# Reordering the first 512 tokens of a fused scan, expert and feed-forward kernel, with dummy matmuls between

## Chip, cores and metric

One core of a Trainium2 chip. The metric is device microseconds of one execution of the program. Engines are named as in the profile: PE (TensorE), DVE (VectorE), ACT (ScalarE), POOL (GpSimd), SP (SyncE, which here only issues DMAs).

## What is computed

```python
# attention-like scan: B, H, S, D = 4, 8, 768, 48
scale = np.minimum(mag, 0.999) / (mag + 1e-06)
for t in range(S):
    new_re = ar * S_re - ai * S_im
    new_im = ar * S_im + ai * S_re
    S_re, S_im = (new_re + kv, new_im)          # kv = outer(k, v)
    y[:, :, t] = np.einsum('bhd,bhde->bhe', q[:, :, t], S_re)
# x: 3072 tokens of 384; E = 4 experts of 1024
for e in range(E):
    h = np.maximum(x @ w1[e], 0.0)
    out += p[:, e:e + 1] * (h @ w2[e])
# second network, hidden 2048
h = x @ w_in
return np.maximum(0.01 * h, h) @ w_out
```

## The kernel before, in words

**Chunks.** The scan is cut into 24 chunks of 128 tokens, six for each batch. A chunk has two generators, and each call of `next` on one issues a few instructions. `elementwise(c)` (L163) has 18 calls: DVE, ACT and POOL turn the decays into running magnitudes (the scans at L198 and L203), running phases (L216) with sine and cosine, and the tile `ft`, the products with q and k (L234, two multiplies). Its last call, `by_head` (L243), issues six DMAs that turn `ft` into `hd`, which has the heads' features in partitions. `products(c)` (L258) has eight calls: PE transposes k (`pt`, L269; copied to `kt`, L270), multiplies scores (`sc`, L280; DVE masks them into `att`, L281), makes the next state (`pm`, L289; DVE writes `st`) and the output (`py`, L301 and, for a chunk with a state before it, L303), which ACT copies to `y` and PE transposes once more (`px`, L311). ACT and DVE then split `px` into `xh` and `xl` (L319, L320), a rounded part and the rest. All small tiles of PSUM here (`pt`, `sc`, `pm`, `py`, `px`) turn through two buffers of one tag, so each waits for the reader of the one before the last.

**Units.** Four chunks are a group of 512 tokens, and six groups go through 32 units of the experts and 16 of the second network. A unit is 128 hidden columns. `gemm_in` (L444) issues nine matmuls into `ph`; DVE makes `hp` (L460), ACT `hh` (L472), DVE `hl` (L473); `gemm_out` (L476) issues nine more into `acc` (L484 to L486). `ph` has three buffers, so a `gemm_in` waits for the `hp` of three units earlier. I call nine matmuls on one set of tokens a piece. Group 0 is special: its first `NHALF` units run on 256 tokens (chunks 0 and 1), then again on the other 256 (chunks 2 and 3), and only the rest on all 512. A unit's weights come raw and are split in two (`wt`): for the first six halves by PE (`rest_early`, two matmuls with the identity, L429 and L430), later by ACT and POOL (L408, L409). SP stores split weights to HBM (`ws`) and reads them back for every later use.

**What sets the order.** Each engine executes its instructions in the order in which they were issued, and that order is written by hand. Before the first unit a string, `PLAN`, is read letter by letter: a digit is one step of that chunk's `elementwise`, `p` and `q` one step of the products of chunks 0 and 1, `s` and `m` the two parts of the early weight split, `n` the normalisation of the expert weights. After it, the unit loop (L609 on) issues for unit number s: `gemm_in` of s + 2, some steps of `background()`, `split_h` of s + 2, `gemm_out` of s, more background steps. `background` finishes the `elementwise` steps of chunks 2 and 3, idles `WAIT` steps, runs the products of chunks 2 (`r`) and 3 (`t`), and goes on with chunk 4 and later. `pace` says how many steps are due by when; `KN` and `E2` set its first slope.

Of the kernel before, what the change touches and what calls it, by code (L numbers as in the profile page):

```python
# [10 lines left out]
F32 = mybir.dt.float32  # L11
# [21 lines left out]
AR_MIN = 0.76  # L33
NHALF = 8
PLAN = (
    "0101001010101011" "01ss0000mm" "00sss11mm000" "1111ppsm23111qq"
    "23232n3pp23p2ppqq3q23qqpq23m"
)
MAXT = 3
KN = 3.0  # L40
PT = 32
TPOOL = 6
MARGIN = 2.0
LAG = 2
E2 = 20
RAWS = 4
# [5 lines left out]
NSTEPS = ESTEPS + len(PSTEPS)  # L52
WAIT = 4
AR_MAX = 1e4
# [7 lines left out]
def fused_kernel(  # L62
# [20 lines left out]
    with ExitStack() as fast:  # L83
# [74 lines left out]
        def table(name):  # L158
            if tables[0] != name:
                A.preload_act_table_set(name)  # L160
                tables[0] = name

        def elementwise(c):  # L163
            t, vt = inputs[c]
# [78 lines left out]
        def by_head(c):  # L243

            ft, vt = feats[c]
            pool = p_el2 if c in (1, 3) else p_el
            hd = pool.tile([2 * D, H, 2 * P + 1], F32, name="hd")
            for ri in range(2):
                for i in range(NG):
                    row = ri * D + i * DG  # L250
                    (A if c < 2 and (i == ri or i == 2 - ri) else SP).dma_start(hd[row : row + DG], ft[:, ri, i])
            feats[c] = (ft, hd, vt)
# [5 lines left out]
        def products(c):  # L258
# [7 lines left out]
            for ri in range(2):  # L266
                pt = ps_a.tile([P, NG, P], F32, name="pt", tag="pa")
                for i in range(NG):
                    PE.transpose(pt[:, i], ft[:, ri, i, P : 2 * P], ident)  # L269
                A.copy(  # L270
                    kt[:, :, ri * D : (ri + 1) * D].rearrange("t h (r d) -> t r d h", d=DG),
                    pt.rearrange("t r (d h) -> t r d h", h=H),
                )
                yield
# [25 lines left out]
            for h in range(H):  # L300
                PE.matmul(py[:, h], att[:, h], vt[:, h * D : (h + 1) * D], start=True, stop=first)  # L301
                if not first:
                    PE.matmul(py[:, h], hd[:, h, :P], old[:, h], start=False, stop=True)  # L303
                if h == 3:
                    yield
# [182 lines left out]

        def zipped(*gens):
            gens = list(gens)  # L490
            while gens:
                for x in list(gens):
                    if next(x, gens) is gens:
                        gens.remove(x)
                yield

        def run_all(*gens):
            gens = list(gens)
            while gens:
                gens = [x for x in gens if next(x, gens) is not gens]  # L500

        with tc.manual_schedule():
# [13 lines left out]
            early_halves = iter([(s, part) for s in range(6) for part in (0, 1)][: PLAN.count("s")])  # L516
            for x in PLAN + "m" * 8:
                if x in steps:
                    next(steps[x], None)
                elif x == "n":  # L520
                    normalise_probs()
                    load_pb(0)
                elif x == "s":
                    cast_early(*next(early_halves))
                elif x == "m":
                    rest_early()
            for s in (5, 6):
                load_unit(s)
            split_unit(3, 0)

            def background():
                for _ in range(2):
                    next(steps["2"])
                    yield
                for _ in zipped(steps["2"], steps["3"]):
                    yield
# [36 lines left out]

            first = 2 + max(0, ESTEPS + 1 - min(PLAN.count("2"), PLAN.count("3"))) + WAIT + E2 - PLAN.count("r") - PLAN.count("t")
            pace = [(0.0, 0), (KN, first)]
# [267 lines left out]
```

## Time and profile before

| | us |
|---|---|
| three runs, median (lowest to highest) | 1477.9 (1477.68 to 1480.69) |
| the profiled execution: its own time | 1478.36 |
| its span in the trace | 1476.6 |
| PE busy in the span | 1402.4 (95%) |
| DVE / ACT / POOL busy | 864.7 / 564.8 / 264.5 |

PE's busy time counts a matmul as busy whether the clock is at its full 2.4 GHz or at 1.2 GHz; the granted clock (PEclk, 1.00 or 0.50) says which. Time is lost for PE both where it stands idle and where it is busy at 0.50.

### The profile page before, as it was taken

The numbers are of one execution on the slowest core, as the hardware profiler recorded it, in microseconds if no ns is written. First come the engines' busy times: TensorE is split into PE (matmuls) and PEld (weight loads), VectorE is DVE, ScalarE is ACT, GpSimd is POOL, SyncE is SP. The second block draws the span as 40 slices with busy tenths as digits, with TensorE's granted clock in tenths as the row PEclk, the third lists the DMA queues.
The fourth block names the chain that finished last, engine by engine and source line by source line (L and its number), as shares of the span: only waits on it lengthen the run. The fifth ranks groups of instructions, "written<-read, shape, count | busy, mean of one in ns | idle before, by whom it ended". The sixth has DMA issues, their size and how long they took to land.

```text
span 1476.6 us, 18540 instructions
## 1 busy us (share of the span) xinstructions
PE 1402.4 (95%) x6978; PEld 1177.2 (80%) x6978; DVE 864.7 (59%) x1504; ACT 564.8 (38%) x961; POOL 264.5 (18%) x244
## 2 busy tenths in 40 slices
PE   3858999999999999999999999999999999999997
PEld 1858888888777888788888888888888888888886
DVE  7556887788988898785454554554443333333332
ACT  5424565444345434455234354233332111323232
POOL 2120565412223223221011110110110000100000
PEclk9569999999999999999999999999999999999999
DMA  7288789986788789588567477576465665556561
GB/s 192 43 207 301 212 255 298 331 291 208 273 301 290 250 305 319 153 303 245 153 234 222 151 242 216 188 222 199 154 199 172 231 207 196 190 188 208 190 212 65
DMA packets 91043, 325.49 MB, mean 220 GB/s; under 512 B 10464, under 2 KB 32064, under 8 KB 90944
## 3 DMA queue, kind: packets, MB, share of 16 engines
q1 hardware_dynamic: 87488, 318.71, 67.1%
q10 hardware_dynamic: 3456, 5.51, 1.3%
q8 instruction: 56, 0.92, 0.3%
q14 instruction: 43, 0.35, 0.1%
HBM read 262.72 MB, written 42.52 MB: 207 GB/s over the span
## 4 chain that ended last, share of the span: by engine, by line
PE 58%; DVE 2%; ACT 0%; issue 0%; DVEq 0%; ACTq 0%
PE ph L455 27%; PE acc L484 9%; PE acc L486 9%; PE acc L485 9%; PE sc L280 1%; PE py L301 1%; PE py L303 1%; PE pm L289 1%; PE pt L269 0%; DVE hl L473 0%; DVE hp L460 0%; PE px L311 0%; DVE d L349 0%; ACT hh L472 0%; DVE d L355 0%
## 5 line engine op out<-in xcount | busy, mean ns | idle before, releaser
L455 PE MATMUL ph<-xh,wt 128*128 128x512 f32 (+1 forms) x1200 | 397.9, 388 | 0.0
L484 PE MATMUL acc<-hh,wt 128*128 128x512 f32 (+1 forms) x888 | 350.8, 395 | 5.2 <-ACT o L604 5.1
L486 PE MATMUL acc<-hl,wt 128*128 128x512 f32 (+1 forms) x888 | 342.9, 386 | 4.5 <-DVE hl L473 4.5
L485 PE MATMUL acc<-hh,wt 128*128 128x512 f32 (+1 forms) x888 | 341.5, 385 | 0.0
L472 ACT CAST hh<-hp 128x512 fp32r<-128x512 f32 (+1 forms) x296 | 180.4, 610 | 418.2 <-DVE hp L460 326.5
L473 DVE TENSOR_TENSOR hl<-hp,hh 128x512 fp32r<-128x512 f32 (+1 forms) x296 | 213.4, 721 | 150.3 <-ACT hh L472 149.1
L455 PEld LDWEIGHTS ph<-xh,wt 128*128 128x128 f32 x1200 | 225.5, 190 | 42.4 <-ACT ge L121 0.3
L460 DVE SCALAR_TENSOR_TENSOR hp<-ph,pb 128x512 f32<-128x512 f32 (+1 forms) x200 | 133.0, 665 | 189.9 <-PE ph L455 188.6
L455 PE MATMUL ph<-xl,wt 128*128 128x512 f32 (+1 forms) x600 | 230.2, 384 | 0.0
L486 PEld LDWEIGHTS acc<-hl,wt 128*128 128x128 f32 x888 | 167.3, 188 | 40.0 <-DVE hl L473 6.0
L455 PE MATMUL ph<-x2h,wt 128*128 128x512 f32 x576 | 198.3, 398 | 0.0
L484 PEld LDWEIGHTS acc<-hh,wt 128*128 128x128 f32 x888 | 167.7, 189 | 36.5 <-ACT o L604 5.8
L485 PEld LDWEIGHTS acc<-hh,wt 128*128 128x128 f32 x888 | 168.0, 189 | 30.7
L463 DVE SCALAR_TENSOR_TENSOR hp<-hp 128x512 f32<-128x512 f32 x96 | 72.0, 750 | 185.0 <-ACT hp L462 184.9
L455 PEld LDWEIGHTS ph<-xl,wt 128*128 128x128 f32 x600 | 114.1, 190 | 20.3 <-DVE xl L320 0.2
L455 PEld LDWEIGHTS ph<-x2h,wt 128*128 128x128 f32 x576 | 108.7, 189 | 25.1
L462 ACT COPY hp<-ph 128x512 f32<-128x512 f32 x96 | 56.3, 586 | 178.5 <-PE ph L455 178.5
L455 PE MATMUL ph<-x2l,wt 128*128 128x512 f32 x288 | 114.5, 397 | 0.0
L409 POOL TENSOR_TENSOR wt<-raw,wt 128x384 fp32r<-128x384 f32 x58 | 65.0, 1142 | 62.4 <-ACT wt L408 62.3
L643 POOL TENSOR_TENSOR x2l<-o,x2h 128x512 fp32r<-128x512 f32 x18 | 25.2, 1424 | 256.4 <-ACT x2h L642 256.4
L301 PE MATMUL py<-vt,att 128*128 128x48 f32 x384 | 70.9, 280 | 0.1
L280 PEld LDWEIGHTS sc<-hd 96*128 96x128 f32 x384 | 54.2, 208 | 15.4 <-issue 7.9
(97 smaller groups left out, 1482.2 us busy)
## 6 DMA issues: line engine op xcount, KB each, us to landing
wt<-ws_scratch SPq DMA_DIRECT2D x264, 768.0 KB, 4.8
ws_scratch<-wt SPq DMA_DIRECT2D x32, 768.0 KB, 7.5
hd<-ft SPq DMA_DIRECT2D x138, 128.5 KB, 5.4
aaqk<-in_attn_dram SPq DMA_DIRECT2D x22, 768.0 KB, 8.9
raw<-in_w_dram SPq DMA_DIRECT2D x32, 384.0 KB, 4.5
r<-in_w_dram SPq DMA_DIRECT2D x32, 384.0 KB, 7.4
ws_scratch<-dw SPq DMA_DIRECT2D x32, 384.0 KB, 6.2
pb<-pn_scratch SPq DMA_DIRECT2D x24, 256.0 KB, 6.5
```

The lines of the kernel that those rows point to most:

```text
L280: PE.matmul(sc[:, j], hd[:, h, P : 2 * P], hd[:, h, :P], start=True, stop=True)
L301: PE.matmul(py[:, h], att[:, h], vt[:, h * D : (h + 1) * D], start=True, stop=first)
L409: G.tensor_tensor(wt[:, 1], raw, wt[:, 0].bitcast(F32), ALU.subtract)
L455: PE.matmul(ph[:, : t1 - t0], wt[:, wi, cols], x[kc][:, t0:t1], start=n == 0, stop=n == 3 * NG - 1)
L460: V.scalar_tensor_tensor(hp, ph, 0.0, pbs[g, u // 8][:, t0:t1], ALU.max, ALU.mult)
L462: A.copy(hp, ph)
L463: V.scalar_tensor_tensor(hp, hp, 0.01, hp, ALU.mult, ALU.max)
L472: A.copy(hh, hp)
L473: V.tensor_tensor(hl, hp, hh.bitcast(F32), ALU.subtract)
L484: PE.matmul(out, wt[:, 0, cols], hh, start=first, stop=False)
L485: PE.matmul(out, wt[:, 1, cols], hh, start=False, stop=False)
L486: PE.matmul(out, wt[:, 0, cols], hl, start=False, stop=last)
```

## The change

`PLAN` is rewritten: it has the same letters for chunks 0 to 3, `p` and `q` (18 steps each of chunks 0 and 1, 8 each of 2 and 3, 8 each of `p` and `q`), with the steps of 2 and 3 at other places, all `m` in the string itself, and four `w`. A `w` issues three dummy matmuls (`warm`): the identity against an input tile, 384 columns, into a PSUM bank that no one reads. Four more stand singly in `py` of chunk 1. `LATER` replaces the even alternation of chunks 2 and 3 after the first unit: chunk 2 has ten of the first thirteen steps. Chunk 1's `kt` copies go from ACT to DVE, and three of its six `hd` DMAs go from ACT's queue to SP's. Ten units instead of eight run on 256 tokens, with the pace constants to match. Line numbers grow by ten to thirteen.

```diff
-NHALF = 8
+NHALF = 10
 PLAN = (
-    "0101001010101011" "01ss0000mm" "00sss11mm000" "1111ppsm23111qq"
-    "23232n3pp23p2ppqq3q23qqpq23m"
+    "0101001010101011" "01ss0000mm" "00sss11mm000" "1111ppsmww23111"
+    "23n22qqw33ppm22p3ppmqqw3q2233qqpq"
 )
+LATER = "23222232232223333333"
-KN = 3.0
+KN = 4.0
-E2 = 20
+E2 = 17
-WAIT = 4
+WAIT = 11
+        def warm(n):
+
+            out = ps_acc.tile([P, TG], F32, name="warm", tag="acc0")
+            for _ in range(n):
+                PE.matmul(
+                    out[:, : NG * P], ident, inputs[0][0][:, 0].rearrange("p g t -> p (g t)"),
+                    start=True, stop=True,
+                )
-                    (A if c < 2 and (i == ri or i == 2 - ri) else SP).dma_start(hd[row : row + DG], ft[:, ri, i])
+                    (A if c == 0 and (i == ri or i == 2 - ri) else SP).dma_start(hd[row : row + DG], ft[:, ri, i])
-                A.copy(
+                (V.tensor_copy if c == 1 else A.copy)(
+                if c == 1 and h % 2:
+                    warm(1)
-            for x in PLAN + "m" * 8:
+            for x in PLAN:
+                elif x == "w":
+                    warm(3)
-                for _ in range(2):
-                    next(steps["2"])
-                    yield
-                for _ in zipped(steps["2"], steps["3"]):
+                for x in LATER:
+                    next(steps[x], None)
                     yield
-            first = 2 + max(0, ESTEPS + 1 - min(PLAN.count("2"), PLAN.count("3"))) + WAIT + E2 - PLAN.count("r") - PLAN.count("t")
+            first = len(LATER) + WAIT + E2
```

PE before, from chunk 0's last early weight split (`ph`) to chunk 0's output (`py`):

```order
L269 MATMUL pt<-ident,ft 128x128 x6
L429 MATMUL ph<-raw,ident 128x384
L430 MATMUL ph<-wt,minus 128x384
L269 MATMUL pt<-ident,ft 128x128 x6
L280 MATMUL sc<-hd 128x128 x8
L289 MATMUL pm<-vt,kt 96x48 x8
```

PE now, the same stretch:

```order
L279 MATMUL pt<-ident,ft 128x128 x6
L441 MATMUL ph<-raw,ident 128x384
L442 MATMUL ph<-wt,minus 128x384
L168 MATMUL warm<-aaqk,ident 128x384 x6
L279 MATMUL pt<-ident,ft 128x128 x6
L168 MATMUL warm<-aaqk,ident 128x384 x3
L290 MATMUL sc<-hd 128x128 x8
L441 MATMUL ph<-raw,ident 128x384
L442 MATMUL ph<-wt,minus 128x384
L299 MATMUL pm<-vt,kt 96x48 x8
```

Six dummies stand ahead of chunk 1's transposes and three ahead of chunk 0's scores; the last early weight split, which stood behind chunk 1's `px`, stands behind chunk 0's scores.

DVE before, after the first three units' `hp`, to chunk 2's `ft` (chunk 2's own tiles are 284 to 289, chunk 3's 293 to 298; the five `ge` and `th` rows of a chunk follow its phase scan):

```order
L216 SCALAR_TENSOR_TENSOR th_298<-ones_104,th_289,tr_294 128x128 x3
L227 COPY ft_288<-ge_286 128x6
L218 TENSOR_SCALAR ge_295<-th_298 128x384
L219 TENSOR_SCALAR ge_295<-ge_295 128x384
L220 TENSOR_TENSOR th_298<-th_298,ge_295 128x384
L460 SCALAR_TENSOR_TENSOR hp_582<-ph_572,pb_340 128x256
L222 TENSOR_SCALAR th_298<-th_298 128x384
L223 TENSOR_SCALAR ge_295<-th_298 128x384
L234 TENSOR_TENSOR ft_288<-cs_287,aaqk_129 128x6x128
```

DVE now, from the fourth unit's `hp` on (chunk 2's `ft` is 296, chunk 3's phase 306):

```order
L485 TENSOR_TENSOR hl_606<-hp_597,hh_605 128x256
L226 SCALAR_TENSOR_TENSOR th_306<-ones_104,th_297,tr_302 128x128 x3
L244 TENSOR_TENSOR ft_296<-cs_295,aaqk_129 128x6x128 x2
L472 SCALAR_TENSOR_TENSOR hp_643<-ph_633,pb_333 128x256
L228 TENSOR_SCALAR ge_303<-th_306 128x384
L229 TENSOR_SCALAR ge_303<-ge_303 128x384
L230 TENSOR_TENSOR th_306<-th_306,ge_303 128x384
L232 TENSOR_SCALAR th_306<-th_306 128x384
L233 TENSOR_SCALAR ge_303<-th_306 128x384
L485 TENSOR_TENSOR hl_658<-hp_643,hh_657 128x256
```

Chunk 3's five rows behind its phase scan, and the fifth unit's `hp` and `hl`, now stand behind chunk 2's `ft`; the fourth unit's `hl` stands ahead of it.

PE, at chunk 2's first products: before, five pieces into `ph` and three into `acc` stand ahead of chunk 2's `pt`; now eight and five. Up to chunk 3's `px` it is eight and five before, ten and eight now.

## Rows read from the trace of the kernel before

**Rows 1.** Page, part 2: TensorE busy tenths in 40 slices of 36.9 us

```profile
PE   3858999999999999999999999999999999999997
```

**Rows 2.** Windows (columns: stretch, length, five engines busy, PEclk, DMA share, GB/s)

```profile
32.60:44.40 11.80, 5.30 (x22) 4.63 (x22) 5.85 (x17) 7.90 (x13) 0.00 (x0) 0.50 0.80 86
44.40:66.70 22.30, 22.23 (x105) 21.04 (x106) 9.34 (x22) 4.06 (x8) 0.00 (x0) 0.50 0.08 30
...
77.50:95.70 18.20, 3.43 (x15) 3.20 (x16) 13.82 (x24) 7.00 (x15) 7.44 (x7) 0.67 0.60 111
95.70:104.20 8.50, 8.50 (x44) 8.50 (x44) 2.83 (x5) 0.00 (x0) 0.00 (x0) 0.50 1.11 222
...
111.10:122.40 11.30, 10.17 (x92) 9.80 (x91) 3.67 (x7) 2.15 (x4) 0.06 (x1) 1.00 1.02 422
122.40:400.00 277.60, 267.18 (x1488) 228.45 (x1487) 225.83 (x389) 142.78 (x250) 108.48 (x99) 0.99 0.83 269
```

**Rows 3.** Timeline, TensorE, 24 to 45 us (start, length, instruction, idle before it)

```profile
24.97 0.81 PE L429 MATMUL ph<-raw,ident 128*128 128x384 f32 x2
...
32.91 1.51 PE L269 MATMUL pt<-ident,ft 128*128 128x128 f32 x6 [3.76 <-DVE ft L234]
36.47 3.79 PE L280 MATMUL sc<-hd 96*128 96x128 f32 x16 [2.04 <-ACT kt L270]
44.47 2.79 PE L289 MATMUL pm<-vt,kt 128*96 128x48 f32 x16 [4.21 <-DVE att L281]
```

**Rows 4.** Timeline of TensorE, 56 to 67 us

```profile
56.50 0.63 PE L301 MATMUL py<-vt,att 128*128 128x48 f32 x2
...
63.33 1.67 PE L311 MATMUL px<-ident,y 128*128 128x128 f32 x6
...
66.74 0.58 PE L455 MATMUL ph<-xh,wt 128*128 128x256 f32 x1
```

**Rows 5.** Timeline of VectorE, 32 to 43 us

```profile
32.68 1.02 DVE L183 TENSOR_TENSOR tb<-ge 128x384 f32<-128x384 f32 x2
39.03 0.56 DVE L185 TENSOR_TENSOR ta<-ta,tb 128x384 f32<-128x384 f32 x1 [5.33 <-ACT ta L121]
...
42.85 0.95 DVE L188 SCALAR_TENSOR_TENSOR cs<-aaqk,ge 128x768 f32<-128x768 f32 x1
```

**Rows 6.** Timeline of ScalarE, 30 to 38 us: its DMA issues

```profile
32.80 2.77 ACTq L251 DMA_DIRECT2D hd<-ft  x3
```

**Rows 7.** Timeline of VectorE, 66 to 86 us

```profile
66.03 2.77 DVE L203 TENSOR_TENSOR_SCAN ge<-ta,ones 128x128 f32<-128x128 f32 x6
...
82.57 0.36 DVE L218 TENSOR_SCALAR ge<-th 128x384 f32<-128x384 f32 x1
...
84.83 0.95 DVE L234 TENSOR_TENSOR ft<-cs,aaqk 128x768 f32<-128x768 f32 x1
```

**Rows 8.** Timeline of TensorE, 86 to 123 us

```profile
86.87 1.51 PE L269 MATMUL pt<-ident,ft 128*128 128x128 f32 x6 [9.38 <-DVE ft L234]
...
95.70 3.75 PE L280 MATMUL sc<-hd 96*128 96x128 f32 x16 [5.40 <-DMA hd<-ft]
...
114.43 1.06 PE L280 MATMUL sc<-hd 96*128 96x128 f32 x8
115.32 1.48 PE L289 MATMUL pm<-vt,kt 128*96 128x48 f32 x16
116.64 0.39 PE L301 MATMUL py<-vt,att 128*128 128x48 f32 x2
...
118.41 0.36 PE L455 MATMUL ph<-xh,wt 128*128 128x256 f32 x1
...
119.56 0.31 PE L301 MATMUL py<-vt,att 128*128 128x48 f32 x2
...
122.01 0.55 PE L311 MATMUL px<-ident,y 128*128 128x128 f32 x3 [0.57 <-ACT y L307]
```

**Rows 9.** Timeline of SyncE's DMA queue

```profile
86.75 7.71 SPq L251 DMA_DIRECT2D hd<-ft  x12
```

More of the change, by code (lines that the diff above doesn't have):

```diff
@@ L486, in gemm_out @@
                 PE.matmul(out, wt[:, 0, cols], hl, start=False, stop=last)
[L489 to L494, printed above, removed]
-                yield
[L497 to L500, printed above, removed]
         with tc.manual_schedule():
@@ L531, in background @@
             def background():
-                for _ in range(2):
-                    next(steps["2"])
-                    yield
-                for _ in zipped(steps["2"], steps["3"]):
+                for x in LATER:
+                    next(steps[x], None)
                     yield
```

## The prediction

> **What bounds the kernel now.** I read the page's slices first: PE is at 9 tenths from the fifth slice to the end, and below it in the first four and the last [rows 1]. So the kernel is bound by PE's work, and what can be gained lies in the first 130 us or so. The windows show how it is lost there, and that it is in two ways [rows 2]. From 44.4 to 66.7 us PE is busy all the time, but at a granted clock of 0.50 (1.2 of 2.4 GHz); from 77.5 to 95.7 it is busy for 3.4 of 18.2 us; from 95.7 to 104.2 it is busy at 0.50 again. From 122.4 to 400 it is busy for 267.2 of 277.6 us at 0.99, so there is little to win behind the start.
>
> The PE timeline names the waits. Chunk 1's transposes wait 3.76 us for `ft`, chunk 0's scores 2.04 us for the `kt` copies of ACT, `pm` 4.21 us for `att` of DVE [rows 3]. DVE is late there because it waited 5.33 us itself for a square of ACT [rows 5], and ACT had spent 2.77 us on issuing three `hd` DMAs before its copies [rows 6]. The first unit starts at 66.74 [rows 4]; I call this T0. Then chunk 2's transposes wait 9.38 us for `ft` and its scores 5.40 us for `hd` [rows 8], and chunk 3's `px` ends at 122.56 (122.01 and its 0.55). At that point all four chunks are done and 13 pieces of units (eight into `ph`, five into `acc`). This is the point against which I measure.
>
> **Step 1, to the first unit.** Two squares (1.02 us) and the expert weights' short instructions stay ahead on DVE [rows 5], and chunk 1's two `kt` copies now stand behind chunk 2's add and flag pass (0.56 and 0.95, same rows). The scores of chunk 0 wait for these copies. What goes is ACT's 2.77 us of DMA issues and 1.45 us of copies, so ACT's squares come some 4 us earlier and DVE no longer waits 5.33 us. Together the copies are done near 37.3 by my addition (32.7, plus 1.0, about 1.4 for the short ones, 0.6, 1.0, and half of the two copies); the bounds are 36.5, as now, and 39. The price of moving the copies is thus some 0.8 us here, against the 4.21 us of `pm` that go.
>
> Dummies: a matmul with the identity on 384 columns takes 0.65 us at full clock (from 24.97 to the next at 25.62, the pair's length being 0.81 [rows 3]) and twice that at 0.50. Nine stand in stretches where PE waits today: 5.9 us, inside the 3.76 and 2.04 of waits and the 2 us around them. They wait for nothing (their input is chunk 0's first load, and no one reads their bank), and the next load into that input's buffer is issued behind the first unit. Seven stand on the path: 4.6 us at full clock, 9.1 at 0.50.
>
> At full clock the rest is priced by chunk 3: scores 0.89 for eight instructions, so 1.8 for a chunk; `pm` 1.3; `py` 1.77 for one half of a chunk with a state, 3.55 for all of it [rows 8]; at 0.50 the same `py` takes 6.8 (56.50 to 63.33 [rows 4]). From 37.3: scores 1.8, early split 1.3, `pm` 1.3, `py` of chunk 0 1.8, scores 1.8, three dummies 1.95, `pm` 1.3, `py` with four dummies 6.15 gives 54.7. From the end of `py` to the first unit it took 3.4 us with the early split in between; without it, with ACT's and DVE's copies as they are, 2.8. **T0 becomes 57.5**, 9.2 us earlier, if the clock stays at 1.00.
>
> Does it stay? In rows of before it fell at 32.6 behind an idle stretch of 3.76 us [rows 2, 3], which six dummies now fill. It stayed at 1.00 through 111.1 to 122.4 [rows 2], where scores, `pm`, `py` and a few pieces alternate with idle times of 0.6 us: that is what the stretch from 37 to 57 will look like. So I take full clock. The bounds: at 0.50 all the way from the scores on, 37.3 plus 3.7, plus the 22.3 us that the window 44.4 to 66.7 took, plus 9.1 for the dummies, is 72.4; with the nine dummies ahead at 0.50 too (another 5.9, of which 0.8 is covered), 77.5.
>
> The Trainium skill ("TensorE: Matmul & The Clock Gate", Why this matters for your kernels) advises to keep TensorE busy without a break to get the full clock. By that rule before's products, 22.2 us busy in 22.3, would have been lifted by themselves, and T0 would come out at 57.5 even if the dummies did little. The trace disagrees: the window shows 0.50 throughout [rows 2], so a stream of products alone does not lift a clock that has fallen, and the sum rests on not letting it fall.
>
> **Step 2, chunk 2 behind the first unit.** DVE is the chain here: chunk 2's `ft` ends at 86.7, 20.0 us after T0. Of what stands ahead of it, the 2.77 us of scans at L203 [rows 7] moves ahead of `xl`; only 0.8 us of it is on the path, since `hp` could not start before one piece. Chunk 3's five short rows go behind `ft`: 82.57 to 84.83 less one `hp`, 1.9 us [rows 7]. One `hl`, 0.4, comes ahead. So `ft` is ready at T0 + 17.7. SP takes 7.71 us to issue the twelve `hd` DMAs of chunks 2 and 3, so 3.9 for a chunk [rows 9], and from first issue to scores it was 8.95 us (86.75 to 95.70): scores at T0 + 26.7. On PE, the fifth unit's `hl` is behind chunk 3's rows, at about T0 + 20.5, and two pieces, the transposes and another piece follow: T0 + 24.6 at full clock, 28.5 at 0.50. I take **T0 + 27.5** for the scores, where before has 28.96. So this wait is not gone; PE has merely done 14 pieces by then, not nine.
>
> From the scores of chunk 2 to chunk 3's `px` the same PE work stands in both kernels (two pieces into `ph`, two into `acc`, the products): 26.9 us before. Some 4.2 us of that were lost to 8.5 us at 0.50 [rows 2], and 1.7 to 3.4 us at the same level behind 107.6. I take back 2.9 of these 5.9: 24 us, with 26.9 and 21 as bounds. Chunk 3 is then done at 57.5 + 27.5 + 24 = 109.0.
>
> **Step 3, more units in the waits.** At that point ten pieces into `ph` and eight into `acc` are done, five more than before. Nine matmuls take 1.15 us (118.41 to 119.56 [rows 8]); at 1.1, five are 5.5 us. Before stands at the same work at 122.6 + 5.5 = 128.1. **The gain is 19.1 us.**
>
> **What is given back.** Two units run as four half pieces each, not two whole ones: 0.5 us, my estimate, as four starts more cost little. Two more stores and reads of 786 KB each are 3.1 MB, 7.5 us at the 422 GB/s of rows 2, on queues that are full from 95.7 to 122.4 (DMA share 1.02 to 1.11). No PE wait on a weight read shows there today, so this costs between 0 and 7.5; I take 1. The same steps of chunks 4 to 8 stand in 26 unit times, not 27, with DVE busy for 81% of the stretch behind 122.4: 0 to 3, I take 1. Chunk 1's `hd` DMAs all on SP land some 2 us later, at about 42.5, and are wanted at 43.5: nothing, 2 us if late. Moves of WAIT, E2 and KN only place background steps; their effect is in these steps.
>
> **Sum.** 19.1 - 2.5 = 16.6 us. The profiled execution took 1478.36; its median neighbour 1477.9 is 0.5 less. 1478.4 - 16.6 = 1461.8: I say **1462**.
>
> **Rivals.**
> *The clock falls in the middle* of the products, for about half of them: T0 near 65, the second part at 26.9: 65 + 54.4 = 119.4, gain 8.7 - 2.5: 1472. For it: `py` and `pm` at 48 columns fall out of 1.00 at 107.6. Against: four dummies among `py`.
> *The dummies are late work (slower).* If the clock is at 0.50 from the first dummies on, PE arrives late everywhere: T0 = 77.5, end 77.5 + 54.4 = 131.9 against 128.1, and with 1 us for the split: 1483. It decides at T0 = 73.7. For it: products alone never lifted the clock. Against: matmuls on the identity with 384 columns ran at 1.00 just before 29 us, and the dummies are the same instruction.
> *Full clock throughout*, `hd` of chunk 2 quicker since chunk 3's no longer follows at once: T0 + 25 + 21 = 103.5, gain 24.6 - 2: 1456.
> *Weight reads late* in the second half of ten units, at the upper bound of 7.5: 1468.
> *It does not do what it says:* both strings have the same eight steps of chunks 2 and 3 before the first unit, so by count nothing is brought forward; only order changes. Then only steps 1 and 3 remain and chunk 2's `ft` stays at T0 + 20: 1464, inside the forecast's own range.
>
> **Numbers.** Forecast with the last rival 0.54 (own range 1458 to 1467), clock falling halfway 0.17, slower 0.08, full clock 0.10, late reads 0.11. What a measurement can tell from no change here is 0.2%, 3 us. Faster by more: all of forecast, full clock and late reads, and most of the halfway case: 0.86. Within 0.2%: 0.06, from between halfway and slower. Slower: 0.08. The range goes from the full-clock case to beyond the halfway case: 1454 to 1474; above it stays some 0.13, below it a few in a hundred.
>
> **What would show it.** T0 (first L467) near 57.5, and PEclk 1.00 from 33 us to there; `pm` of chunk 0 without a wait of 4 us. Chunk 2's `ft` at T0 + 17.7, its scores at T0 + 27.5 still waiting for `hd` or `hl`; an idle stretch of 4 to 5 us before the fifth unit's `acc`. Chunk 3's `px` near 109 with 18 pieces done. PE's idle time behind 130 us as before, some 20 us. I am wrong if PEclk falls to 0.50 in the products, if PE waits on `wt` from `ws` behind 110 us, or if the gain at 128 us is seen in the trace and the end does not move with it.

## The result: 0.6% slower, though the first unit comes 10 us earlier

The changed kernel takes 1490.52 us in the median of six runs (1485.32 to 1491.78), the kernel before 1479.3 beside it (1476.91 to 1483.56): 1.0064 of it, 95% interval 1.0045 to 1.0083. I had said 1462. The profiled execution took 1489.17, its span is 1487.5, 10.9 us longer than before's.

The page's slices, part 2 (busy tenths of PE, and under them the granted clock in tenths):

```profile
PE   4859999999999999899999999999999999999997
...
PEclk9968999999999999999999999999999999999999
```

The third slice, 74 to 112 us, has 5 tenths as it had before the change [rows 1]; the loss is still at the start. The windows after the change, cut at the new landmarks (the columns of [rows 2]):

```profile
32.60:44.40 11.80, 10.19 (x70) 8.05 (x69) 9.76 (x25) 7.50 (x14) 0.00 (x0) 1.00 0.86 99
44.40:56.80 12.40, 11.79 (x83) 9.62 (x82) 7.59 (x17) 3.28 (x8) 2.34 (x2) 1.00 0.20 74
56.80:77.00 20.20, 15.04 (x99) 13.89 (x99) 17.33 (x29) 7.79 (x16) 9.92 (x9) 0.83 0.40 129
77.00:99.40 22.40, 6.64 (x33) 5.86 (x34) 8.44 (x16) 5.66 (x13) 6.29 (x6) 0.65 1.06 259
99.40:104.20 4.80, 4.80 (x25) 4.80 (x25) 1.81 (x3) 1.24 (x3) 1.84 (x2) 0.50 1.01 421
...
122.40:400.00 277.60, 263.22 (x1487) 225.32 (x1486) 217.43 (x376) 137.51 (x240) 107.47 (x93) 0.99 0.81 263
```

Up to 56.8 us all is as forecast: the clock is at 1.00 and PE works 22 of 24.2 us, where it had been at 0.50 or idle. Then come 22.4 us (77.0 to 99.4) in which PE works 6.6, while the DMA engines are full (share 1.06). Behind 122.4 PE does 4 us less than before. PE's timeline, from chunk 1's transposes to chunk 2's scores:

```profile
33.20 0.82 PE L279 MATMUL pt<-ident,ft 128*128 128x128 f32 x6
...
36.99 2.05 PE L290 MATMUL sc<-hd 96*128 96x128 f32 x16 [1.04 <-DVE kt L280]
...
40.17 1.48 PE L299 MATMUL pm<-vt,kt 128*96 128x48 f32 x16
...
55.38 0.82 PE L323 MATMUL px<-ident,y 128*128 128x128 f32 x6
56.82 0.38 PE L467 MATMUL ph<-xh,wt 128*128 128x256 f32 x1 [0.62 <-ACT xh L331]
...
83.77 0.83 PE L279 MATMUL pt<-ident,ft 128*128 128x128 f32 x6
...
99.40 1.86 PE L290 MATMUL sc<-hd 96*128 96x128 f32 x7 [13.73 <-ACT kt L280]
```

The waits of 3.76 and 4.21 us of [rows 3] are gone and the first unit is 9.9 us earlier than in [rows 4]. The wait of 9.38 us for `ft` in [rows 8] is gone too. But chunk 2's scores start 3.7 us later than before: they wait 13.73 us for the `kt` copies. ACT's timeline says why the copies are late:

```profile
81.92 0.92 ACT L420 CAST wt<-raw 128x384 fp32r<-128x384 f32 x2
84.44 0.41 ACT L484 CAST hh<-hp 128x256 fp32r<-128x256 f32 x1 [1.60 <-DVE hp L472]
97.72 0.92 ACT L420 CAST wt<-raw 128x384 fp32r<-128x384 f32 x2 [12.87 <-DMA ws_scratch<-wt]
98.55 1.47 ACT L280 COPY kt<-pt 128x384 f32<-128x384 f32 x2
```

ACT stands before a weight split of unit 9, behind which the copies are queued. The split writes a `wt` buffer, of which there are seven. Units 0 to 6 take them all; unit 7 takes unit 0's and unit 8 unit 1's. Unit 0's second turn, for which `load_split` runs just before `split_unit`, takes unit 2's, so unit 9 gets unit 3's, and that one is free only when unit 3's weights have been stored to `ws`. SyncE's queue shows when that was:

```profile
77.08 3.78 SPq L261 DMA_DIRECT2D hd<-ft  x6
80.91 0.59 SPq L625 DMA_DIRECT2D ws_scratch<-wt  x1
82.93 3.80 SPq L261 DMA_DIRECT2D hd<-ft  x6
86.83 0.54 SPq L151 DMA_DIRECT2D aaqk<-in_attn_dram  x1
87.61 0.33 SPq L155 DMA_DIRECT2D vt<-in_v_dram  x1
88.75 1.32 SPq L625 DMA_DIRECT2D ws_scratch<-wt  x2
```

Unit 3's store is the first of the two at 88.75, behind chunk 3's `hd` and chunk 4's loads; such a store takes 9.2 us to land (median of four in this stretch), and ACT's split starts 9.0 us after this one was issued. With eight units the last split is unit 7's and takes the buffer of unit 1.

Chunk 3's `px` ends at 128.78 with 18 pieces done, where the kernel before has done the same work at 128.1 in its own trace too. So the whole gain is gone there. As a measure behind it I take the start of ACT's `hh` cast of the same unit in both traces: at unit 10, the first that both kernels run on all 512 tokens, the changed kernel is 1.0 us ahead, at unit 28 5.3 behind, at the end 10.8. So it also loses 11.8 us behind 160 us; the windows place part of that (before first, then the change; PE busy, clock):

```profile
200.00:290.00 90.00, 88.77 (x478) 1.00 0.92 292
```

```profile
200.00:290.00 90.00, 84.40 (x448) 0.96 0.84 273
```

### The profile page after: what moved, and what is told of

It reads as the page before. It is cut to its first block, busy times and chain, and to the rows that moved or that the text cites. A ratio compares the mean times of both kernels' runs of the same rounds, so it can differ in the third digit from the quotient of the medians.

```text
span 1487.5 us, 18678 instructions
## 1 busy us (share of the span) xinstructions
PE 1410.9 (95%) x7046; PEld 1179.8 (79%) x7046; DVE 873.1 (59%) x1510; ACT 564.1 (38%) x961; POOL 270.7 (18%) x244
## 4 chain that ended last, share of the span: by engine, by line
PE 57%; issue 0%; ACT 0%; DVE 0%
PE ph L467 26%; PE acc L496 9%; PE acc L498 9%; PE acc L497 9%; PE sc L290 1%; PE py L311 1%; PE py L313 1%; PE pm L299 1%; PE pt L279 0%; PE px L323 0%; DVE hp L475 0%; ACT o L603 0%; ACT hh L484 0%; ACT hp L474 0%; ACT dw L369 0%
## 5 line engine op out<-in xcount | busy, mean ns | idle before, releaser
L485 DVE TENSOR_TENSOR hl<-hp,hh 128x512 fp32r<-128x512 f32 (+1 forms) x298 | 218.5, 733 | 164.2 <-ACT hh L484 161.7
L467 PEld LDWEIGHTS ph<-xh,wt 128*128 128x128 f32 x1212 | 228.5, 191 | 44.0 <-ACT xh L331 1.7
L496 PEld LDWEIGHTS acc<-hh,wt 128*128 128x128 f32 x894 | 170.1, 190 | 44.1 <-ACT hh L484 7.6
L497 PEld LDWEIGHTS acc<-hh,wt 128*128 128x128 f32 x894 | 170.6, 191 | 31.1
L290 PE MATMUL sc<-hd 96*128 96x128 f32 x384 | 54.9, 291 | 21.8 <-ACT kt L280 14.0
L311 PE MATMUL py<-vt,att 128*128 128x48 f32 x384 | 67.3, 267 | 2.4 <-DVE att L291 2.4
```

What stands on the lines that cost most here:

```text
L290: PE.matmul(sc[:, j], hd[:, h, P : 2 * P], hd[:, h, :P], start=True, stop=True)
L467: PE.matmul(ph[:, : t1 - t0], wt[:, wi, cols], x[kc][:, t0:t1], start=n == 0, stop=n == 3 * NG - 1)
L485: V.tensor_tensor(hl, hp, hh.bitcast(F32), ALU.subtract)
L496: PE.matmul(out, wt[:, 0, cols], hh, start=first, stop=False)
L497: PE.matmul(out, wt[:, 1, cols], hh, start=False, stop=False)
```

## Experiments

Theory A: the stall at unit 9's split. Theory C: the later loss comes from E2, 17 instead of 20. In the kernel before 33 steps really stand ahead of chunk 4's and 36 are counted, a lead of three; after the change 48 stand there and 48 are counted. Rivals: the dummies cost, or the clock. Each run has one line, with the run that it is built on and its edit; those without one are the changed kernel with the edit. T0 is the first unit, "scores" the start of chunk 2's, "px" the end of chunk 3's; "first" and "end" are the `hh` casts of unit 10 and of the last unit against before's, minus being earlier. All these are from the profiled execution, which lies up to 5 us from the median of its runs (e11's, e15's and e16's are the slowest of theirs, e14's is 5 us below its median). The ratio is that of the timed runs to the kernel before:

| run | T0 | scores | px | first | end | ratio (95%) |
|---|---|---|---|---|---|---|
| before | 66.74 | 95.70 | 122.56 | 0 | 0 | 1 |
| after | 56.82 | 99.40 | 128.78 | -1.0 | +10.8 | 1.0064 (1.0045 to 1.0083) |
| e1 swap | 58.59 | 90.94 | 119.71 | -6.4 | +5.5 | 1.0009 (0.9996 to 1.0022) |
| e2 lead | 57.09 | 99.86 | 132.17 | +6.4 | +7.4 | 1.0022 (1.0009 to 1.0036) |
| e3 no dummies | 56.78 | 100.66 | 130.86 | +2.6 | +11.5 | 1.0063 (1.0041 to 1.0085) |
| e4 before, ten | 66.69 | 95.53 | 128.53 | +1.8 | +3.3 | 1.0001 (0.9989 to 1.0014) |
| e5 swap, lead | 60.36 | 92.72 | 122.87 | -1.8 | +1.4 | 0.999 (0.9977 to 1.0002) |
| e6 before, E2 17 | 66.81 | 95.82 | 121.93 | -4.8 | +3.2 | 1.0022 (1.0003 to 1.004) |
| e7 e5, no dummies | 62.44 | 96.21 | 119.47 | -6.0 | -3.3 | 0.998 (0.9965 to 0.9995) |
| e8 `kt` on DVE | 58.65 | 89.08 | 130.97 | +1.2 | +12.6 | 1.0051 (1.0033 to 1.007) |
| e9 e7, eight units | 56.40 | 86.81 | 115.32 | -4.7 | -5.0 | 0.994 (0.9921 to 0.9959) |
| e10 e7, two queues | 54.49 | 87.66 | 113.68 | -10.5 | -9.1 | 0.9947 (0.9927 to 0.9967) |
| e11 e7, E2 23 | 62.12 | 96.04 | 124.90 | +6.2 | +19.2 | 1.0082 (1.0065 to 1.0099) |
| e12 e7 again | 56.76 | 90.42 | 120.83 | -3.1 | -0.4 | 0.9979 (0.9963 to 0.9995) |
| e13 e10, dummies | 56.90 | 89.03 | 117.74 | -6.6 | -3.7 | 0.9966 (0.9948 to 0.9984) |
| e14 e9, two queues | 56.81 | 86.67 | 109.99 | -9.7 | -9.2 | 0.9949 (0.9929 to 0.9969) |
| e15 e9, dummies | 60.29 | 89.18 | 117.59 | -2.4 | -2.3 | 0.9931 (0.9916 to 0.9947) |
| e16 after, eight, lead | 60.02 | 88.91 | 117.30 | -2.6 | -2.2 | 0.9938 (0.9921 to 0.9954) |
| **e17 after, eight** | 56.84 | 85.75 | 110.12 | -15.8 | -8.1 | **0.9927** (0.9915 to 0.9939) |

e1 to e4, e5 to e8, e9 to e11, e12 to e15 and e16 with e17 each share a chip.

### The stall

**e1** ("swap"), `load_split` behind the splits, so that unit 9 takes unit 2's buffer:

```diff
-                load_split(s + 5)
                 load_pb(s + 6)
                 split_unit(s + 4, 0)
                 split_unit(s + 3, 1)
+                load_split(s + 5)
```

> The changed kernel with the weight reload of unit s+5 issued behind the two splits of the loop's top, not ahead of them, so that unit 9 takes the buffer of unit 2 and not that of unit 3. Theory A (the stall): unit 9's cast on ScalarE waits until unit 3's store has landed at 97.8 us, because that store stands on SyncE's queue behind chunk 3's six hd DMAs; chunk 2's kt copies stand behind that cast, and TensorE waits 13.7 us for them. Unit 2's store landed at 87.8, so chunk 2's scores should start near 89.5, not 99.4, TensorE's wait there should fall from 13.7 to 4 us or less, and the whole should end 8 to 11 us earlier: 1479 to 1482, ratio to before 1.000 to 1.002. Rival B (the DMA engines): hd, store and load share the engines, which were full from 86 to 105 us; then something else waits for a landing near 97 us, the scores start at 96 or later and the time stays at 1487 or more.

Measured 1483.53, 1.0009. ACT's timeline:

```profile
89.25 0.93 ACT L420 CAST wt<-raw 128x384 fp32r<-128x384 f32 x2 [2.64 <-DMA ws_scratch<-wt]
90.08 1.50 ACT L280 COPY kt<-pt 128x384 f32<-128x384 f32 x2
```

The split waits 2.64 us instead of 12.87, and the scores start at 90.94. Theory A holds for 0.55%, 8 us; the later loss stays, 11.9 us from "first" to "end".

The swap shortens the stall and does not end it. PE's timeline puts the wait of the scores down to `hd`, but chunk 2's six `hd` transfers were issued from 78.85 to 82.05 and took at most 5.4 us to land, so all had landed by 87.5. What came last was the first `kt` copy, behind the split, which now waits for unit 2's store. So it is in every run with ten units and the swap (e1, e5, e7, e10 to e13): the scores start 0.05 us after the first `kt` copy and 3.0 to 3.7 us after the last `hd`. With eight units it is the other way about: the first copy has been done for 3.5 to 4 us, and the scores start 0.1 us after the last `hd`.

**e8**, the stall left, but chunk 2's copies on another engine:

```diff
-                (V.tensor_copy if c == 1 else A.copy)(
+                (V.tensor_copy if c in (1, 2) else A.copy)(
```

> The changed kernel with the two transposed-key copies of chunk 2 on DVE instead of ACT; unit 9's split still waits for unit 3's store. Theory A (the scores of chunk 2 are late because their copies stand behind that split on ACT's in-order queue): the scores of chunk 2 start at 86 to 91 us instead of 99.4, though the split still waits until about 97 us; what stands behind it on ACT (the cast of unit hidden halves, y of chunk 2) then waits instead, so that of the 9 us that the swap saved some 3 to 8 come back: 1483 to 1488 us. Rival (the split itself, not the copies behind it, holds the path: units run out before 97 us): the scores move but the products of chunk 3 end as late as in the changed kernel, near 128 us, and the time is 1489 to 1492 us.

Measured 1489.05, 1.0051; the rival was right. DVE's timeline shows where the wait went:

```profile
88.23 1.46 DVE L280 COPY kt<-pt 128x384 f32<-128x384 f32 x2
100.87 0.60 DVE L485 TENSOR_TENSOR hl<-hp,hh 128x256 fp32r<-128x256 f32 x1 [11.18 <-ACT hh L484]
101.39 1.27 DVE L291 TENSOR_TENSOR att<-sc,causal 128x512 f32<-128x512 f32 x2
```

The scores come 10.3 us earlier, but a unit's `hh` stands behind the same split on ACT, its `hl` heads DVE's queue, and chunk 2's mask (`att`) is behind that. Two in-order queues hand the one late store on; the split itself, and not only the copies behind it, holds the path.

**e4**, ten units in the kernel before, with its own order:

```diff
-NHALF = 8
+NHALF = 10
-KN = 3.0
+KN = 4.0
-WAIT = 4
+WAIT = 11
```

> The kernel before with ten units on 256 tokens and no other part of the change (KN = 4 and WAIT = 11 go with the ten; E2 stays 20): no dummies, PLAN, LATER, kt copies and DMA queues as before. Theory A: here chunk 2's kt copies stand ahead of unit 9's cast on ScalarE, so it is chunk 2's y copy that waits for unit 3's store; some stall of 5 to 12 us appears between chunk 2's scores and its px, and the ten units gain little: 1476 to 1484, ratio 0.998 to 1.004. Rival F: the loss of the changed kernel comes from the reordered PLAN and LATER, not from the ten units; then there is no new wait of ScalarE for a store here, and the time is 1470 to 1475.

Measured 1480.96, 1.0001: in the old order ten units neither cost nor win. The stall is there as well, as theory A expected. Chunk 2's copies stand ahead of unit 9's split on ACT, so chunk 2's `y` copy is late, and PE waits for it before `px`:

```profile
111.16 0.92 ACT L408 CAST wt<-raw 128x384 fp32r<-128x384 f32 x2 [16.34 <-DMA ws_scratch<-wt]
```

```profile
112.51 0.90 PE L311 MATMUL px<-ident,y 128*128 128x128 f32 x3 [7.86 <-ACT y L307]
```

So the net price, 20 us below, belongs to ten units together with the new order.

### The lead of the background steps

**e2**, the changed kernel with E2 20.

```diff
-E2 = 17
+E2 = 20
```

> The changed kernel with E2 = 20, not 17: every background step from chunk 4 on is due three steps earlier against the units, as it was before. Theory C (lost lead): the 7 us that the changed kernel loses against the one before between whole units 22 and 31 of group 0 (205 to 283 us), where scores wait for hd and for a cast, come from that lead; then this loss should fall to 2 us or less, the stall at chunk 2's scores stay at 13 to 14 us, and the time should be 1482 to 1485, ratio 1.002 to 1.004. Rival D: the loss comes from the steeper pace or from the same elementwise work being crowded by DMA traffic, and stays; then the time is 1487 to 1491.

Measured 1484.12, 1.0022. Only 1 us is lost behind unit 10 (+6.4 to +7.4), as theory C says; but that unit is 7.3 us later than after the change. The net is 6 us in the median.

**e6**, the other way about, E2 17 in the kernel before (the same line, 20 to 17).

> The kernel before with E2 17 instead of 20, nothing else. Theory C (the later loss is the missing lead of three background steps, whatever the order of the first 512 tokens): the steps of every later chunk come three steps later, a loss opens between 200 and 290 us and another near 600 to 660 us as in the changed kernel, 5 to 10 us in all: 1486 to 1490 us. Rival (the loss belongs to the new order, where chunk 4's arrays and the unit weights land later): within 2 us of the kernel before, 1479 to 1483 us.

Measured 1481.54, 1.0022 with an interval that begins at 1.0003, and an expectation that was too high. The three steps make unit 10 some 5 to 7 us earlier or later (e6; e5 against e1; e2) and move the loss behind it by 8 to 11 us the other way; what remains is small here.

**e5**, e1 and e2 together.

> The changed kernel with both repairs: load_split(s + 5) behind the two split_unit calls (unit 9 takes unit 2's weight buffer, not unit 3's) and E2 back to 20 (background steps three further ahead). Theory 'two separate losses' (A: the stall of ACT at unit 9's split; C: the three missing steps of lead): the first saves the 9 us it saved alone (scores of chunk 2 at about 91 us), the second the 6 to 7 us lost behind 130 us, but three steps more of work lie before the first 130 us; the first whole unit is 0 to 5 us earlier than in the kernel before, nothing is lost behind it, and the time is 1474 to 1481 us, below the kernel before. Rival (the gain is taken back wherever it is made, since the work on 256 tokens that is moved ahead is only borrowed): the difference to the kernel before creeps back to +3 to +6 us by 300 us, and the time is 1483 to 1487 us.

Measured 1479.53, 0.999: both repairs add up, as the first theory said, though the intervals of e1 and e5 still overlap. But 0.1% was all that the new order then seemed worth.

**e11**, E2 23, in e7 (below).

> The run with both repairs and no dummies, with E2 23 (six background steps ahead, not three). Theory C as the runs have it so far (three steps of lead cost 5 to 7 us before 170 us and bring back 8 to 10 us behind 200 us; with three steps nothing more is lost behind 300 us): the early cost comes a second time and nothing is left to bring back, so the first whole unit is 3 to 7 us later and the time 1480 to 1485 us. Rival (each further step of lead still brings 1 us net): 1472 to 1476 us.

Measured 1492.66, 1.0082. The early cost came a second time, at twice the size (unit 10 is 12.2 us later than in e7), and 13.0 us more were lost behind it in the profiled execution, which neither theory had; that execution is 5 us slower than the median.

### The dummies

**e3**, the changed kernel without them:

```diff
-            for _ in range(n):
+            for _ in range(0 * n):
```

> The changed kernel without any of the 16 dummy matmuls; all else is the same. Theory A says that the dummies do what they should (first unit at 56.8 us, not 66.7) and that what they win is lost again in the stall, whose end is set by DMA landings behind chunk 2's features. Without them the clock should fall near 32 us, the products run at 0.50, the first unit start at 62 to 66 us, and chunk 2's scores still start within 5 to 10 us behind 99.4; the time 1493 to 1498, ratio 1.010 to 1.013. Rival E: the dummies are 10 us of TensorE work that costs its time; then the time is shorter than the changed kernel's, 1480 to 1487.

Measured 1490.72, 1.0063: the same as with them. T0 is the same too (56.78), although the clock was at 0.50 from 32.0 to 42.3 and from 52.5 to 62.7. That was a miss: the earlier first unit is the work of the order, not of the dummies.

**e7** is e5 without them, **e12** the same kernel on another chip.

> As the run with both repairs, and every dummy matmul taken out. Theory 'dummies fill waits that nothing hangs on': within 2 us of the run with both repairs (the TensorE clock is at 0.50 in two stretches before 65 us as in the run without dummies, and the first unit comes at the same time). Rival (the lower clock costs where the products of chunks 2 and 3 are next): 4 to 8 us more than the run with both repairs.

> The run with both repairs and no dummies once more, as the reference of the three that follow on the same chip. If the gain of the two-queue and eight-unit runs is theirs: again 0.996 to 0.9995 of the kernel before (1475 to 1480 us). Rival (they differed only in what clock the first 70 us were granted): 0.994 to 0.996, as they had.

Measured 1477.72 and 1476.79, 0.998 and 0.9979. The windows of e7 show what the dummies are there for (columns: stretch, length, PE busy, clock, DMA share, GB/s):

```profile
47.00:54.00 7.00, 6.69 (x35) 0.50 0.08 31
54.00:57.00 3.00, 3.00 (x16) 0.50 0.00 0
57.00:67.00 10.00, 9.42 (x41) 0.50 0.00 0
```

The same stretch of e10, also without dummies:

```profile
47.00:54.00 7.00, 6.70 (x61) 1.00 0.07 25
54.00:57.00 3.00, 2.50 (x10) 0.56 0.00 0
57.00:67.00 10.00, 9.29 (x73) 0.96 0.33 118
```

Without dummies the products of this stretch may run at 0.50 (T0 62.44) or at 1.00 (T0 54.49), and which of the two comes is not in the program: e12, the same kernel as e7, has T0 at 56.76. What the dummies do shows over all profiles of the new order. In the seven without them the clock falls to 0.50 between 31.7 and 33.9 us; in the nine with them it falls at 43.8 or later. T0 lies between 54.5 and 62.4 without dummies; with them it is 56.8 to 57.1 where the clock holds up to the first unit (four profiles) and 58.6 to 60.4 where it falls at 43.8 to 44.8 (five). So they cost some 2.3 us where the clock stays (my estimate from 56.82 after the change and 54.49 in e10) and take off the late end.

**e13** has dummies and, as e10, chunk 2's `hd` on two queues:

> Both repairs, chunk 2's hd transfers on two queues, and the dummies in. Theory 'the dummies are an insurance': without them the first unit came between 54.5 and 62.4 us as the granted clock fell or not; with them between 56.8 and 60 us. So the median is within 3 us of the two-queue run without dummies (0.9947 of the kernel before), with a smaller spread. Rival (the dummies cost what they occupy, some 3 us of TensorE before the first unit, and win nothing): 3 to 5 us more, 0.997 or above.

Measured 1475.72, 0.9966 against 0.9947: within the 3 us of "insurance", if only just; e15 against e9 goes the other way (0.9931 and 0.994). In four pairs (e3, e7, e10 and e9 against the run with them) the dummies moved the median by -0.1 to +0.2%: no effect that these runs can tell from none.

### Two queues for `hd`

**e10**, in e7, and **e14**, in e9 (the text of e10 miscounts: it is three of chunk 2's six transfers):

```diff
-(A if c == 0 and (i == ri or i == 2 - ri) else SP)
+(A if c in (0, 2) and (i == ri or i == 2 - ri) else SP)
```

> The run with both repairs and no dummies, with four of chunk 2's twelve hd transfers (six stores, six loads counted as one row each here: those with i == ri or i == 2 - ri) issued by ACT and not SP, as chunk 0's are. Theory 'the scores of chunk 2 wait for hd because SP issues one transfer in 0.65 us': SP is through 1.3 to 2.6 us earlier, hd lands 1 to 3 us earlier, the wait of 3.2 us before the scores goes, and the time falls by 0 to 3 us: 1474 to 1478 us. Rival (the 16 DMA engines are the limit: one hd transfer lands about 1 us after the one before it whoever issues it, and ACT's issues delay its copies by 2 to 3 us): hd lands within 1 us of before, ACT's kt copies are late instead, and the time is 1477 to 1481 us.

> Eight units on 256 tokens, both repairs, no dummies, and chunk 2's hd transfers on two queues: the two edits that were each faster. If what they save adds up (the eight-unit run waited 9.0 us for chunk 2's ft before its key transposes and 5.2 us for hd behind them; two queues take 2 to 3 us off the second): 0.991 to 0.993 of the kernel before, 1467 to 1470 us. Rival (with eight units the wait for ft takes back what hd gives, since units run out): 0.993 to 0.996.

Measured 1470.91 and 1474.27, 0.9947 and 0.9949: e10 faster than either expectation, e14 in the rival's range, so the two edits do not add up. With ten units the scores wait for ACT's `kt` copies and not for `hd` (see e1): they start 12.0 us after the first transfer was issued with two queues (e10, 75.69 to 87.66) and 11.9 with one (e12, 78.53 to 90.42). The pair with eight units decides, where they do wait for `hd`: 8.69 us with two queues (e14, 77.98 to 86.67), 8.71 with one (e9, 78.10 to 86.81). So the scores gained nothing. The Trainium skill ("DMA: Bandwidth & Descriptors", Issuing engines are not separate DMA queues) says that a second issuing engine saves only the time of issuing; the trace agrees, SyncE being done in 1.84 us (e14) instead of 3.78 (e9). With ten units the median came out 0.2 to 0.3% lower in both pairs, with eight it did not; where those would come from I can't show.

### Ten units

**e9**, eight units again, in e7:

```diff
-NHALF = 10
+NHALF = 8
-KN = 4.0
+KN = 3.0
-WAIT = 11
+WAIT = 0
```

> The run with both repairs and no dummies, with eight units on 256 tokens again (NHALF 8, and WAIT 0 and KN 3 that the shorter stretch needs; the lead of three background steps stays). Theory 'ten units are needed because the units must last until chunk 3's products are done': the first units run out before them, PE waits 5 to 10 us for chunk 3's y between 115 and 130 us, and the time is 1483 to 1489 us. Rival (the two extra units only stretch the stage; the products of chunk 3 end in time for eight): no new wait above 2 us, and 1475 to 1480 us, as with ten.

Measured 1472.12, 0.994: the units did not run out before chunk 3's products, as the rival said, and the time is below its range too.

**e15**, the same with the dummies.

> The eight-unit run with the dummies in. By 'insurance': within 3 us of the eight-unit run without them (0.994). By 'dummies cost': 3 to 5 us more, 0.9965 to 0.998.

Measured 1471.52, 0.9931, as "insurance" said.

**e16** is the changed kernel with the three numbers of e9 and E2 20, and **e17** with the three alone:

> The changed kernel with four numbers altered and no code: NHALF 8 (with the WAIT 0 and KN 3 of the shorter stretch) and E2 20. Its order of the first 512 tokens and its dummies stay, and load_split stays ahead of the two split_unit calls. Theory 'the order of the first 512 tokens is worth what its earlier first unit says, and the ten units and the missing lead take it back': unit 7, the last that is split here, takes the buffer of unit 1, whose store has long landed, so ACT waits for none; the time is that of the eight-unit run with the swap, 0.992 to 0.995 of the kernel before, 1469 to 1475 us. Rival (the swap is needed with eight units too): a wait of over 3 us on ACT ahead of chunk 2's key copies, and 1476 to 1482 us.

> As the run beside it, with E2 17 as the change has it: the ten units alone are undone. By the price that the missing three steps of lead had so far (3 to 6 us in the median: 3 us in the kernel before, 6 and 3 us in the changed one without and with the swap): 3 to 6 us more than the run beside it, 1473 to 1480 us. Rival (the lead matters only where ten units have pushed the later steps back): within 2 us of it.

Measured 1471.85 and 1469.87, 0.9938 and 0.9927, as the theory of e16 and the rival of e17 said: faster than both kernels, and e17 differs from the changed one in three constants. The lead is worth nothing here: in the median e16 and e17 agree, though in the profiles e17 is 15.8 us ahead at unit 10 and 8.1 at the end, e16 2.6 and 2.2 (e16's is its slowest execution). PE's timeline in e17:

```profile
56.84 0.38 PE L467 MATMUL ph<-xh,wt 128*128 128x256 f32 x1 [0.62 <-ACT xh L331]
...
77.19 0.88 PE L279 MATMUL pt<-ident,ft 128*128 128x128 f32 x3 [9.49 <-DVE ft L244]
79.78 0.84 PE L279 MATMUL pt<-ident,ft 128*128 128x128 f32 x3
85.75 3.75 PE L290 MATMUL sc<-hd 96*128 96x128 f32 x16 [5.12 <-DMA hd<-ft]
...
109.22 0.90 PE L323 MATMUL px<-ident,y 128*128 128x128 f32 x3 [0.57 <-ACT y L319]
```

and ACT's, where no store is waited for and the copies run between the splits:

```profile
80.09 0.91 ACT L420 CAST wt<-raw 128x384 fp32r<-128x384 f32 x2
80.91 0.81 ACT L280 COPY kt<-pt 128x384 f32<-128x384 f32 x1
81.61 0.41 ACT L484 CAST hh<-hp 128x256 fp32r<-128x256 f32 x1
81.92 0.83 ACT L280 COPY kt<-pt 128x384 f32<-128x384 f32 x1
```

The waits for `ft` and `hd` are as long as before the change (9.38 and 5.40 [rows 8]); chunk 2 simply starts 9.9 us earlier.

Two things were not taken apart. NHALF was only ever altered together with WAIT and KN, so "ten units" means the three; WAIT puts chunk 2's products, and so its `kt` copies on ACT, later in the order, and ten units with a shorter WAIT did not run. Nor were the parts of the new order (the string, `LATER`, the copies on DVE, the queue of `hd`) undone one by one, so which of them makes the first unit earlier is open.

## Why the prediction was wrong

Against the sum, chunk 3's `px` came 19.8 us late (128.78, 109.0 said): T0 was 0.7 early, the way from there to chunk 2's scores 15.1 too long, and the way on to `px` 5.4. Behind it 10.2 us were given back in the trace, where I had 2.5.

**Step 1 was right, for half a wrong reason.** Chunk 0's scores came at 36.99 (37.3 said), the first unit at 56.82 (57.5). But "the sum rests on not letting it fall" did not hold: e3 and e12 came to 56.78 and 56.76 with the clock at 0.50 for parts of the way. Nor does "a stream of products alone does not lift a clock that has fallen" hold beyond the one trace: in e3 it was back at 1.00 at 42.3 without a dummy. A clock at 0.50 from 33.3 us on, but for 43.6 to 47.0, gives 62.44 (e7), against 63.3 by my bound (72.4 less the 9.1 us of dummies).

**Step 2.** Chunk 2's `ft` was done at about T0 + 20.2 (its `hd` is issued at 77.08), not T0 + 17.7: none of the forecast 2.3 us was won. The two groups of phase scans on DVE alone took 6.07 us instead of 4.54. The scores came at T0 + 42.6, not T0 + 27.5. I had gone through DVE, SyncE and PE for what stands ahead of them, and not through ACT, the engine that the diff puts nothing on. With the stall shortened by the swap it was T0 + 32.1 to 33.9 with ten units, still held by ACT; T0 + 28.9 to 30.4 with eight and four pieces less, held by `hd`, as before the change (T0 + 28.96). From scores to `px` I said 24, with 26.9 and 21 as bounds: 24.4 in e17, 29.4 after the change, for the same 176 matmuls (see below).

**Step 3.** 18 pieces were done at chunk 3's `px`, as counted. That they come at no cost was wrong: e12, with the swap, has its 18 at 120.83, and e17 14 at 110.12, which with four pieces at 1.1 us is 114.5 (T0 is the same in both).

**The step that failed is "What is given back"**: "Two units run as four half pieces each, not two whole ones: 0.5 us", and "Two more stores and reads of 786 KB each ... I take 1"; and with it the path of step 2, which a late store lengthened. Undoing the ten units (with their WAIT and KN) takes 1490.52 to 1469.87, by the ratios 1.37% or 20 us. The stall was not in the sum at all: I looked for a PE wait on a weight read, and the wait was ACT's, for a store's landing, to get a buffer back. The swap takes off 8 of the 20 us (e1). Of the other 12 some 3 go with E2 (e5 against e1), which costs nothing with eight units. The last 9 are there with both repairs made (e15 against e5, 0.59%; without dummies e9 against e7, 0.4% or 6 us). Up to 3.5 us of these are what the swap leaves of the stall (scores at T0 + 32.4 in e5, T0 + 28.9 in e15). Behind unit 10 the ten-unit runs with E2 20 (e2, e5, e7, e10, e12, e13) lose 1.0 to 3.2 us, the eight-unit ones (e9, e14, e15, e16) -0.4 to +0.5. The rest is not settled; the granted clock, which differs between the profiles, hides it.

**"Moves of WAIT, E2 and KN only place background steps"**, 1 us in the sum: three steps of E2 moved the median by 6 us (e2) and some 3 us (e6, e5 against e1) for ten units or the old order, and by nothing that can be told in e17 against e16. After the change PE worked 4.4 us less than before between 200 and 290 us.

**With eight units most of the gain is there, but not by step 2.** e17 takes 0.73% or 11 us less than before, where I had said 16.6 for ten units. At chunk 3's `px` it has done 14 pieces at 110.12, and before has these at 123.5: 13.4 us, of 19.1 said. They are the 9.9 us of step 1 and 2.5 us between scores and `px`, and one piece more; the waits of step 2 gave nothing. That e17 is 15.8 us ahead at unit 10 says less, since E2 17 alone brings that unit 4.8 us forward (e6) and it is lost again behind.

**Rivals.** The slower case was to come from dummies as late work, deciding at T0 = 73.7; in no run of the new order did T0 pass 62.44. Slower came by another way. "Weight reads late" looked at the right cause, the two units more, and had neither mechanism nor size: it was a store, and ahead of the second half. "It does not do what it says" was right in what it said: chunk 2's `ft` stayed at T0 + 20 (20.2 after the change and in e17), and only steps 1 and 3 remained. Its 1464 left out the price of ten units as the forecast did.

## What to carry to other kernels

Where a change makes a loop of units longer or shorter, write down for each unit whose buffer it gets and which transfer gives it back; one more unit can reach a buffer whose store has not been issued yet. Then look at what stands behind the waiting instruction on its in-order engine, also when the change doesn't touch that engine. Compare the releaser that a trace names with the time at which it was done: after the swap `hd` was named, and had landed 3.7 us before. And when a bundle of edits comes out slower, undo the constants first: three numbers separated a loss of 0.6% from a gain of 0.7%.

## What was not expected of the hardware

The stretch from chunk 2's scores to chunk 3's `px` has the same matmuls on PE in all runs of the new order, and its length goes with the mean granted clock (e8, which waits inside it, apart). The windows of e14, e17, e13 and e2, each from its scores to its `px` (columns as above):

```profile
86.67:109.99 23.32, 21.79 (x176) 0.91 1.05 322
```

```profile
85.75:110.12 24.37, 22.84 (x176) 0.85 1.05 324
```

```profile
89.03:117.74 28.71, 27.31 (x176) 0.70 0.96 339
```

```profile
99.86:132.17 32.31, 30.91 (x176) 0.62 0.64 221
```

That is 9 us between two executions of the same work with PE busy for 93 to 96% of the time in each, nearly as much as e17 gains in all; a single profile of this stage says little of 5 us, and only the medians tell. A store of 768 KB that is issued behind `hd` transfers and loads took 9.2 us to land (median of four, after the change, 86 to 100 us) at full DMA engines.
